# Masks first, small transfers last, turned rows before shifted copies, router steps put off, and weights requested in eight pieces, in a fused attention and expert kernel

## The chip, the cores and the metric

The kernel runs on one core of one Trainium2 chip. The metric is device time in microseconds (us) of one execution. The engines are PE (TensorE matmul; PEld is its weight load), DVE (VectorE), ACT (ScalarE), POOL (GpSimd) and SP (SyncE, which here only issues transfers). L445 is line 445 of the kernel before.

## The reference, cut to what matters

Sliding-window causal attention (8 batches, 8 heads, 576 positions, head width 64, window 64) gives x of 4608 rows by 512. Then each row goes through one of 8 experts.

```
scores = scale * matmul(q, k.T); mask = (rel >= 0) & (rel < 64)
x = softmax(scores masked) @ v            # (8, 576, 512)
logits = x @ w_gate; local = sigmoid(x @ w_local)
for each batch b, in order of s:
    fresh = argmax(logits[b, s])
    e = fresh if s == 0 or local[b, s] < 0.5 else the expert of s - 1
    p = softmax(logits[b, s])
    out[b, s] = p[e] * (relu(x[b, s] @ w1[e]) @ w2[e])
```

The expert of a row depends on the rows before it, so the router scans along the positions, counts the rows of each expert and gives every row a place in a table; the experts then gather their rows by that table.

## The kernel before, in words

**Attention** works through 9 chunks of 512 rows (`sc`), each with 4 units (`hp`, a pair of heads): 36 units, numbered here from 0 to 35. A unit has scores (PE, L389, 36 instructions, into PSUM `sp`), an exponential (ACT, L420), a multiplication by a mask (DVE, L425), values (PE, L435, 32 instructions, into PSUM `xo`), and a normalization on DVE (reciprocal L440, gates L443 in the later chunks, rows `x` L445). Scores run two units ahead of values (`LEAD = 2`). For seven units around chunks 4 to 6 (`BIASED`) a matmul adds the mask to the scores instead, and DVE has no L425. The values need two layouts of v: `va` as loaded and `vb`, shifted by 64 rows, which POOL (L365, L369) and ACT (L364, L367, L371) copy a chunk ahead (`shift`, a generator that gives one piece at a time); for chunk 0 `shift_first` does so in two halves (L379, L380). In chunks 0 to 3 PE turns the finished rows (L306), ACT copies them (L309), and a gate matmul (L319) with L336 and L342 gives the logits `lt`. In chunks 4 to 8 (`GATED`) the gates ride along with the values instead: `gates` and `spread` (L321, L336, L350 to L352) put them beside v. The gates, `spread` and the router share one PSUM bank, `r`.

**Order.** Inside attention the order on PE, ACT and SP is the order written (`manual_schedule`); DVE and POOL are ordered by the framework's scheduler, which may take a later instruction earlier when its data are ready in the scheduler's own model. `issue_after(x)` holds instructions of an engine behind x on that engine.

**Loads.** SP issues all loads. The first chunk's keys, queries and v come first; `until(i, x)` is a tiny transfer that reads x and so holds SP's queue until x is written: the second chunk's loads stand behind `until(0, mask 0)`, the third's behind the first reciprocal. POOL begins with seven small transfers (L117 to L134: gate weights, and zero rows for two DRAM tables), then the iotas for the masks (L260, L267). Mask 0 is built by L279 before the scores of unit 0 are masked, mask 1 behind the masking of unit 1. PE fills its waits at the outset with 12 and then 24 transposes of the identity (L253).

**Router.** `Router.first` handles the first 14 blocks of 128 rows, and runs inside attention from unit 18 on. It is a generator; each `yield w, trip` gives the weight of the step just done and whether the next begins on PE. Every unit has two places for a step (`step()`, ahead of the values and behind them). A place lowers `pause` by 0.8, and when it is at or below zero one step is taken and its weight added. At two places of a unit group (unit 3's first and unit 2's second), where the PSUM bank is in use, a step that begins on PE is not taken. Its steps in order: argmax (L803 to L817), transposes (L823) and a scan along the rows (L828, L829), transposes (L833, L834), carries (L844, L846), experts (L856, L860), counting matmuls (L869, L870) and sums (L872 to L899), the first experts' limits, places (L1040 to L1047 and L928 to L940), and a table: one-hots `rowh` (L968), `one`, `colh`, matmuls (L991), and the row numbers `idx` and `gx` (L993 to L1000). Then POOL gathers the first expert's rows (`ex.rows`, L1176). `Router.second` handles the rest during the first experts; L1126 belongs to it.

**Hand-over.** At the end of unit 27 SP gets the first expert's w1 (four pieces of 512 KB, behind `until(2, ...)`), at the end of unit 29 its w2 (four pieces, behind `until(3, ...)`). After attention PE turns the gathered rows (L1249), ACT copies them (L1250), and the first expert begins (L1473, then L1377). DVE forms sums of w2 (L1290) during its first product.

## Time and profile before

| what | value |
|---|---|
| time, median of 3 runs | 634.47 us (633.39 to 634.62) |
| the profiled execution, its own time | 635.46 us |
| its span, first to last instruction | 633.2 us |
| mean granted TensorE clock | 0.991 |
| PE, PEld, DVE, ACT, POOL busy | 605.1, 532.2, 403.8, 200.8, 271.1 us |
| first expert's first product | 136.43 us |

How to read the lines that follow. A timeline row has: start, duration (us), engine, line, operation, out<-in, shape, xcount, and in brackets the idle time of the engine just before it and what released it. A row that stands for several instructions gives the time from the first to the last. A row of the grouped view has: line, engine, operation, out<-in, xcount | busy us, mean ns | idle us ahead of the group, by releaser. A window row has: from:to, its length, busy us of the engine asked for (xinstructions), granted clock of PE, share of the DMA engines' time, GB/s. "issue" means that nothing the profile shows was waited for.

### The profile page before, as it was taken

How to read it: one execution, taken by the hardware profiler on the slowest of the kernel's cores; microseconds unless marked ns; L12 is line 12 of the kernel's file. 1: busy time of each engine (PE TensorE's matmuls, PEld its weight loads, DVE VectorE, ACT ScalarE, POOL GpSimd, SP SyncE). 2: the span in 40 equal slices, each digit the busy share in tenths (PEclk: the TensorE clock that was granted, in tenths of full speed). 3: DMA queues.
4: the chain of work that ended last, by engine and by line, in shares of the span. 5: the costliest groups of instructions: out<-in, count | busy, mean ns of one | idle time of the engine just before them, and what ended most of it. 6: DMA issues, size and time to landing. Idle time of an engine off the chain costs nothing. (4 is left out here: it accounts for less than half of the span.)

```text
span 633.2 us, 14966 instructions
## 1 busy us (share of the span) xinstructions
PE 605.1 (96%) x6271; PEld 532.2 (84%) x6271; DVE 403.8 (64%) x757; ACT 200.8 (32%) x368; POOL 271.1 (43%) x261
## 2 busy tenths in 40 slices
PE   8889998989999999999999999999999999999994
PEld 7667776878889998979898889888997998989983
DVE  6767579868996767347472785273928752986630
ACT  3756655722382231203130223022211221213120
POOL 5332112525003753446077836182477264574101
PEclk9999989989999999999999999999999999999998
DMA  8999996967945566486967866688689456966401
GB/s 317 412 419 403 382 361 250 322 255 252 376 151 193 194 224 240 168 292 242 384 253 250 293 219 226 212 314 298 275 289 333 182 193 239 370 244 225 166 18 39
DMA packets 31880, 165.79 MB, mean 262 GB/s; under 512 B 10532, under 2 KB 12218, under 8 KB 22587
## 3 DMA queue, kind: packets, MB, share of 16 engines
q1 hardware_dynamic: 20394, 135.54, 57.7%
q0 software_dynamic: 11408, 29.20, 13.1%
q8 instruction: 51, 0.84, 0.5%
q14 instruction: 27, 0.21, 0.1%
HBM read 145.52 MB, written 19.59 MB: 261 GB/s over the span
## 5 line engine op out<-in xcount | busy, mean ns | idle before, releaser
L1176 POOL DMA_INDIRECT xg<-xs,g x118 | 132.9, 1126 | 36.0 <-issue 34.1
L1453 POOL DMA_INDIRECT out_dram<-y,idx x36 | 41.7, 1158 | 179.4 <-DVE y L1386 113.6
L1377 PE MATMUL hp<-ws,hs 128*128 128x256 f32 x384 | 88.9, 380 | 0.0
L1377 PEld LDWEIGHTS hp<-ws,hs 128*128 128x128 f32 x384 | 72.5, 190 | 10.9 <-issue 1.2
L1327 PE MATMUL hp<-xs,ws 128*128 128x128 f32 x672 | 79.7, 275 | 0.0
L1327 PEld LDWEIGHTS hp<-xs,ws 128*128 128x128 f32 x672 | 77.3, 192 | 0.1
L1473 PE MATMUL hp<-xt,w 128*64 128x64 f32 (+2 forms) x640 | 66.2, 276 | 0.0
L1473 PEld LDWEIGHTS hp<-xt,w 128*128 128x128 f32 (+1 forms) x640 | 60.8, 170 | 4.1 <-issue 0.7
L1386 DVE SCALAR_TENSOR_TENSOR y<-hp,pws,kept 128x256 f32<-128x256 f32 x48 | 22.1, 480 | 63.2 <-issue 38.0
L1377 PE MATMUL hp<-w,h 128*128 128x256 f32 x256 | 60.5, 379 | 0.0
L1338 DVE TENSOR_TENSOR h<-hp,keep 128x512 f32<-128x512 f32 x42 | 28.5, 689 | 44.0 <-PE hp L1327 43.9
L1327 PEld LDWEIGHTS hp<-xt,w 128*128 128x128 f32 x448 | 53.2, 192 | 2.7 <-issue 2.3
L1327 PE MATMUL hp<-xt,w 128*128 128x128 f32 x448 | 54.7, 275 | 0.0
L435 PE MATMUL xo<-vb,p 128*64 128x74 f32 (+1 forms) x576 | 46.2, 235 | 8.2 <-DVE x L445 3.5
L1377 PEld LDWEIGHTS hp<-w,h 128*128 128x128 f32 x256 | 47.3, 190 | 5.7
L420 ACT ACTIVATE p<-sp 128x512 f32<-128x512 f32 x72 | 39.2, 595 | 38.5 <-PE sp L389 36.4
L1176 POOL DMA_INDIRECT pws<-xw,gx x40 | 45.4, 1134 | 12.2 <-issue 11.9
L435 PEld LDWEIGHTS xo<-vb,p 128*64 128x64 f32 x576 | 40.6, 143 | 11.0 <-issue 3.8
L389 PEld LDWEIGHTS sp<-w 64*64 64x64 f32 x1296 | 38.6, 137 | 13.3 <-issue 9.8
L425 DVE TENSOR_TENSOR p<-p,mask 128x1024 f32<-128x1024 f32 x29 | 36.4, 1258 | 17.3 <-ACT p L420 17.0
L389 PE MATMUL sp<-w 64*64 64x128 f32 (+1 forms) x1296 | 43.9, 269 | 3.3 <-issue 2.6
L435 PE MATMUL xo<-va,p 128*64 128x74 f32 (+1 forms) x576 | 46.3, 235 | 0.6 <-issue 0.6
(287 smaller groups left out, 966.1 us busy)
## 6 DMA issues: line engine op xcount, KB each, us to landing
w<-in_w_dram SPq DMA_DIRECT2D x22, 2048.0 KB, 9.2
w<-in_w1t_dram SPq DMA_DIRECT2D x20, 2048.0 KB, 8.9
w<-in_kq_dram SPq DMA_DIRECT2D x17, 1024.0 KB, 8.7
w<-in_w_dram SPq DMA_DIRECT2D x24, 512.0 KB, 8.4
xs<-x POOLq DMA_DIRECT2D x9, 1024.0 KB, 7.3
va<-in_v_dram SPq DMA_DIRECT2D x5, 1184.0 KB, 8.0
vtt<-in_vt_dram SPq DMA_DIRECT2D x5, 1024.0 KB, 10.6
va<-in_v_dram SPq DMA_DIRECT2D x3, 1040.0 KB, 13.1
```

The costliest lines, as they stand in the source:

```text
L389: nc.tensor.matmul(sp[j][c * WIN:(c + 1) * WIN, a:b], lhsT=kt[h, hp, block * WIN:(block + 1) * WIN], rhs=qt[h, hp, a:b], start=not biased, ...
L420: nc.scalar.activation(p[:, j], sp[j], Act.Exp, scale=DH ** -0.5)
L425: masked.append(nc.vector.tensor_tensor(p, p, m.to_broadcast([P, 2, SC]), op=Alu.mult))
L435: nc.tensor.matmul(xo[par * WIN:(par + 1) * WIN, j, s * VW:s * VW + n], lhsT=p[:, j, b * WIN:(b + 1) * WIN], rhs=w[:, s, 2 * hp + j, :n], ...
L1176: return self.nc.gpsimd.indirect_dma_start(out=out, out_offset=None, in_=table[:rows, :], in_offset=bass.IndirectOffsetOnAxis(ap=idx, axis=0))
L1327: nc.tensor.matmul(out[:, m, :], lhsT=a[:, kk, m * P:(m + 1) * P], rhs=b[:, kk, :], start=start and m + kk == 0, stop=stop and (m, kk) == ...
L1338: nc.vector.tensor_tensor(o, x, y, op=add)
L1377: nc.tensor.matmul(out, lhsT=a[:, m, :], rhs=b[:, m, :], start=start and m == 0, stop=stop and m == FK // 2 - 1, skip_group_check=True)
L1386: nc.vector.scalar_tensor_tensor(y[i][:, j * w:(j + 1) * w], x, pw[i], y2, Alu.mult, Alu.add)
L1453: self.nc.gpsimd.indirect_dma_start(out=self.out[:, :], out_offset=bass.IndirectOffsetOnAxis(ap=st["idx"][:, s:s + 1], axis=0), in_=y, in_ ...
L1473: nc.tensor.matmul(hp[a, i, :], lhsT=st["w1"][:, kk, m * P:(m + 1) * P][:, a], rhs=st["xt"][:, kk, :n], start=(kk == 0), stop=(kk == DK - 1))
```

## The change: what it does

- **Small transfers.** The seven transfers of POOL go into a function `small()`, called behind unit 2's values and held behind the second half of `shift_first`'s POOL copy.
- **Masks.** Both masks are built at once, ahead of the first scores; `shift_first(0)` stands behind the scores of unit 0 instead of unit 1; the second warm-up has 6 transposes instead of 24.
- **Turned rows.** At unit 0 of chunks 1 to 4 the pieces of `shift` are issued behind the turned rows and their copy, not ahead of them.
- **Router steps.** The scan's step weighs 2.4 instead of 1.5; the second place of unit 3 of a group no longer takes a step that begins on PE; the one-hot `rowh` is made in two halves with a step each; L1126 is held behind attention's last normalization.
- **Weights.** The first expert's w1 goes out in pieces behind units 27, 28, 29 and 30, its w2 behind units 32, 33, 34 and 35, each piece behind that unit's reciprocal.

```diff
@@ kernel
-    nc.gpsimd.dma_start(out=wg2s, in_=wg2)
-    nc.gpsimd.dma_start(out=wgs, in_=wg)
...
-        for i in (ZR, N + 1):
-            nc.gpsimd.dma_start(out=xs[0][i:i + 1, :], in_=zeros[:1])
-            nc.gpsimd.dma_start(out=xw[i:i + 1, :], in_=zeros[:1, :PW])
-        nc.gpsimd.dma_start(out=xw[T1:ZR, :].rearrange("(c p) o -> p c o", p=HF),
-                            in_=zeros[:HF, :n * PW].rearrange("p (c o) -> p c o", c=n))
+        def small():
+            nc.gpsimd.dma_start(out=wgs, in_=wg)
+            nc.gpsimd.dma_start(out=wg2s, in_=wg2)
...
@@ attention
-    build_mask(0)
+    for i in range(2):
+        build_mask(i)
...
     for u in units[:LEAD]:
         ps[u] = scores(*u)
-    shift_first(0)
-    with tc.issue_after(masked[-1].ins):
-        build_mask(1)
-    warm(24)
+        if u == units[0]:
+            shift_first(0)
+    warm(6)
...
-        for _ in range(2 if sc else 4):
-            next(moves, None) if moves else None
+        late_moves = hp == 0 and sc and sc - 1 not in GATED
+
+        def move():
+            for _ in range(2 if sc else 4):
+                next(moves, None) if moves else None
+
+        if not late_moves:
+            move()
...
+        if late_moves:
+            move()
...
-            shift_first(1)
+            second = shift_first(1)
...
+        if i == 2:
+            with tc.issue_after(second.ins):
+                small()
...
-            ex.jobs = [ex.weights({"plain": True}, -1, ("w1",), lambda: until(2, allr[:1, sc, hp, 0, :1]))]
+            ex.jobs = [ex.weights({"plain": True}, -1, (), lambda: until(2, allr[:1, sc, hp, 0, :1]))]
+            ex.piece(ex.jobs[0], "w1", 0)
...
-        step(not (hp == 2 and sc + 1 in GATED))
-        if (sc, hp) == (NSC - 2, 1):
-            ex.weights(ex.jobs[0], -1, ("w2",), lambda: until(3, allr[:1, sc, hp, 0, :1]))
+        step(not (hp >= 2 and sc + 1 in GATED))
+        at = i - (len(units) - 2 * HP)
+        if 0 <= at < 2 * HP and at != HP - 1:
+            until(3 + at, allr[:1, sc, hp, 0, :1])
+            ex.piece(ex.jobs[0], "w1" if at < HP else "w2", at % HP + (at < HP))
@@ Router.gate
-        yield 1.5, True
+        yield 1.5 if part else 2.4, True
@@ Router.table
-                    vec.tensor_tensor(rowh, self.io128.to_broadcast(sh), last(lo[:, b:b + m]).to_broadcast(sh),
-                                      op=Alu.is_equal)
-                    yield 0.15 * m, False
+                    for c in range(0, m, PIECE // 2):
+                        d = min(c + PIECE // 2, m)
+                        sh = [P, d - c, P]
+                        vec.tensor_tensor(rowh[:, c:d], self.io128.to_broadcast(sh),
+                                          last(lo[:, b + c:b + d]).to_broadcast(sh), op=Alu.is_equal)
+                        yield 0.15 * (d - c), False
@@ Router.second
-        vec.tensor_scalar(none, self.rank[:, :C1], 0.0, float(2 * N), Alu.is_lt, Alu.mult)
+        with self.tc.issue_after(self.norm.ins) if self.norm else nullcontext():
+            vec.tensor_scalar(none, self.rank[:, :C1], 0.0, float(2 * N), Alu.is_lt, Alu.mult)
@@ Experts
+    def piece(self, st, name, i):
+        w, a, b = (self.w1[0], DK, F) if name == "w1" else (self.w2, FK, D)
+        if not i:
+            t = self.ring.tile([P, a * b], F32, name="w")
+            st[name] = t.rearrange("p (a b) -> p a b", a=a)
+        m = a // PARTS
+        src = w[bass.ds(st["e"], 1)].rearrange("o p (a b) -> (o p) a b", a=a)
+        self.nc.sync.dma_start(out=st[name][:, i * m:(i + 1) * m], in_=src[:, i * m:(i + 1) * m])
```

## The prediction, made before the changed kernel was run

> **What bounds the kernel now.** I began with the page.

> ```profile
> span 633.2 us, 14966 instructions
> ...
> PE 605.1 (96%) x6271; PEld 532.2 (84%) x6271; DVE 403.8 (64%) x757; ACT 200.8 (32%) x368; POOL 271.1 (43%) x261
> ```

> TensorE (PE) is busy for 96% of the span, so there is little to win in all; a change pays only where PE stands still. The chain of waits, read next, is of no help: it covers only the kernel's tail. The edits lie in the attention stage and its hand-over to the first expert, so I grouped PE's instructions of the first 137 us by line and read what ended their waits.

> ```profile
> L435 PE MATMUL xo<-vb,p 128*64 128x74 f32 (+1 forms) x576 | 46.2, 235 | 8.2 <-DVE x L445 3.5 <-issue 3.0 <-ACT p L309 1.5
> ```

> The last column is the idle time ahead of the group, by releaser. PE does its scores (L389) and values (L435) in one written order, so these waits add up one behind the other. Three names matter: the normalization on DVE (3.5), ACT's copy of turned rows (1.5), and "issue" (3.0), where nothing that the profile shows was waited for. In time order the waits that the edits touch are these:

> ```profile
> 15.09 1.12 PE L389 MATMUL sp<-w 64*64 64x128 f32 x36
> 16.50 1.54 PE L389 MATMUL sp<-w 64*64 64x128 f32 x36 [0.29 <-DMA w<-in_kq_dram]
> ...
> 83.22 0.39 PE L823 MATMUL r<-ident,vk 128*14 128x128 f32 x2 [0.55 <-ACT va L352]
> ...
> 85.59 0.17 PE L833 MATMUL r<-ident,loc 14*1 14x14 f32 x1 [0.94 <-DVE loc L828]
> ...
> 104.96 0.28 PE L435 MATMUL xo<-vb,p 128*64 128x74 f32 x1 [2.53 <-DVE x L445]
> ...
> 130.64 0.28 PE L435 MATMUL xo<-vb,p 128*64 128x74 f32 x1 [2.03 <-issue]
> ...
> 136.43 3.94 PE L1473 MATMUL hp<-xt,w 128*128 128x256 f32 x17
> ```

> The last row is the first expert's first product; where it starts is my yardstick, since from there PE hardly pauses. The windows show a second cost of a pause, the granted clock (PEclk):

> ```profile
> 86.00:90.00 4.00, 4.00 (x75) 0.57 0.98 395
> 130.00:134.00 4.00, 3.36 (x57) 0.57 0.95 382
> ```

> Behind the two pauses at 83 to 86 us, and behind the one that ended at 130.64, the clock was 0.57 over 4 us: 4 x 0.43 = 1.7 us lost each time. Behind the longest pause, which ended at 104.96, it stayed at 1.00 (the row from 101 to 111, below).

> **The outset.** The seven small transfers leave the front of GpSimd's queue, both masks are built before the first scores are masked, and 18 of 36 warm-up transposes go.

> ```profile
> 2.46 0.61 POOL L119 DMA_DIRECT2D wgs<-in_wg_dram  x1
> ...
> 5.73 0.15 POOL L260 IOTA row<- 128x1 int32 x1
> ```

> ```profile
> 7.32 2.57 DVE L279 TENSOR_SCALAR mask<-p,rowf 64x512 f32<-64x512 f32 x4
> ...
> 12.35 2.59 DVE L279 TENSOR_SCALAR mask<-p,rowf 64x512 f32<-64x512 f32 x4
> ```

> Six of the seven run back to back from 2.46 to 5.73, so the iota for the masks comes at least 3.3 us earlier. Mask 0 then starts near 4.0 and both masks, of 2.6 us each, end near 9.2, where mask 0 alone ended at 9.9, and mask 1 no longer sits between the first masking and the first normalization. The first values could start up to 2 us sooner, but the row at 16.50 says what is late next: the scores of unit 4 wait for the second block of keys and queries. Its request is released by the first mask, so it goes out earlier too.

> ```profile
> 10.00:14.00 4.00, 4.00 (x86) 1.00 1.00 340
> 14.00:18.00 4.00, 3.68 (x112) 1.00 1.01 428
> ```

> Were the queue kept as full from 10 to 14 us as behind it (428 GB/s for 340), it would carry 0.35 MB more, worth 0.8 us; and unit 4's 36 matmuls, 1.54 us at 16.50, took 1.12 in the unit before, 0.4 less. Together -1.2 us; the ends are 0 (the queue moves what it moves) and -2.1 (the masks' gain whole). I take the DMA row, since it bounds last. The small transfers now stand behind GpSimd's second copy, ahead of this one:

> ```profile
> 18.99 1.04 POOL L365 COPY vb<-va 64x1040 f32<-64x1040 f32 x1 [4.93 <-DMA va<-in_v_dram]
> ```

> GpSimd idled 4.93 us there and the seven take about 3.9 (3.3 for six, and one more like the first's 0.61): nothing. Their first user, the gates of chunk 0, comes a chunk later. Without that cover this copy would be late, and with it unit 4's values, one for one.

> **Turned rows first.** In chunks 1 to 4 ACT now copies the turned rows (L309) before the shifted values (L364, L367). Example:

> ```profile
> 56.25 0.63 ACT L364 COPY vb<-va 64x520 f32<-64x520 f32 x1
> 56.78 1.17 ACT L367 COPY vb<-va 64x1184 f32<-64x1184 f32 x1
> 57.98 1.01 ACT L309 COPY p<-xo 128x1024 f32<-128x1024 f32 x1
> ```

> L309 moves 1.7 us ahead, more than any of the waits of L435 on it, whose sum is 1.5 us. The exponentials behind the three copies start when they did; the shifted values are needed only a chunk later. -1.5 us (0 to -1.5).

> **Router steps put off.** Each unit of attention has two places where the router may take a step; a step's weight is worked off at 0.8 a place. Weight 2.4 instead of 1.5 for the scan, and no PE step at either place late in a unit group, move the first transposes (L823) from behind chunk 4's last values to the next chunk, and L833 a whole unit behind them. Both PE waits go, and the slow clock behind them: 0.55 + 0.94 + 1.7 = 3.2; I leave 0.5 for a wait on the scan: -2.7 us (-0.5 if the clock falls elsewhere, to -3.2).

> Counting places through to the end, the counting matmuls move from before unit 22's values to behind unit 24's, and the table's matmuls (L991) from before unit 29's values to before unit 32's. Here DVE must be weighed.

> ```profile
> 93.65 0.39 DVE L872 COPY sums<-r 128x224 f32<-128x224 f32 x1
> ...
> 100.22 1.18 DVE L1126 TENSOR_SCALAR none<-rank 128x112 f32<-128x112 f32 x1
> ...
> 118.33 0.17 DVE L1000 TENSOR_SCALAR gx<-at 128x6 uint32<-128x6 f32 x1
> 118.41 1.22 DVE L425 TENSOR_TENSOR p<-p,mask 128x1024 f32<-128x1024 f32 x1
> 119.54 0.20 DVE L440 RECIPROCAL allr<-xo 128x8 f32<-128x8 f32 x1
> ...
> 120.52 1.22 DVE L425 TENSOR_TENSOR p<-p,mask 128x1024 f32<-128x1024 f32 x1
> ```

> From the first to the third of these rows DVE does 48 router instructions; start to next start they sum to 11.0 us. L1126 (1.1) is now kept behind the last normalization, and about 1.0 comes after the table: 8.9 are left to do between unit 24's values and the table. In that stretch DVE also has 7 normalizations of 0.98 (119.54 to 120.52) and 5 maskings of 1.13 (118.41 to 119.54), and two reductions:

> ```profile
> L538 DVE TENSOR_REDUCE lt<-g 128x36 f32<-128x288 f32 x2 | 1.3, 668 | 0.0
> ```

> 8.9 + 6.9 + 5.7 + 1.3 = 22.8 us. PE takes

> ```profile
> 101.08 0.41 PE L404 MATMUL sp<-bias,unit 64*64 64x512 bf16 x4
> ...
> 125.98 0.28 PE L435 MATMUL xo<-va,p 128*64 128x74 f32 x1
> ```

> 24.9 us now from the end of unit 24's values to unit 32's, 22.4 without the wait of 2.53. So DVE becomes the bound of this stretch. When it led before,

> ```profile
> 101.00:111.00 10.00, 9.43 (x30) 1.00 0.57 216
> ```

> it was busy 94%: 22.8 / 0.943 = 24.2, so -0.7 us of the 2.5 (ends -2.5, PE's bound, and +1.5, the same again the other way with DVE idling a tenth). Halving the one-hot (L968) adds one start and lets a normalization in between; that lies inside this bound.

> **The hand-over.** The table gives the first expert's row numbers, which GpSimd gathers.

> ```profile
> 118.79 1.78 POOL L1176 DMA_INDIRECT xg<-xs,gx  x1 [2.61 <-DVE gx L1000]
> 120.88 1.74 POOL L1176 DMA_INDIRECT xg<-xs,gx  x1 [0.30 <-issue]
> ```

> ```profile
> w<-in_w_dram SPq DMA_DIRECT2D x24, 512.0 KB, 8.4
> ...
> xg<-xs,g POOLq DMA_INDIRECT x118, 3.3
> ```

> ```profile
> 115.89 0.51 PE L991 MATMUL r<-colh,rowh 128*128 128x12 bf16 x14
> ```

> ```profile
> 134.96 1.07 ACT L1250 COPY xt<-tp 128x512 f32<-128x512 f32 x2 [5.53 <-issue]
> ```

> Now: table done 116.40, indices 118.50 (2.1 later), second gather issued 120.88 (+2.4), landed 3.3 later as such gathers do, or up to 8.4 as a weight piece does (I take 5.0, nearer the row of the same kind), turned and copied (+1.1). That sums to 10.6 us behind the table, and unit 32's values follow the table at once. Before, this chain ended by 128 and hid under units 29 to 35. PE now takes 136.43 - 125.98 = 10.45 us from unit 32's values to the first expert, of which 10.45 - 2.03 - 1.7 = 6.7 are work, so it will wait 3.9 us at the end: 10.6 instead of 10.45, +0.2 us (-1.6 with a landing of 3.3, +3.6 with 8.4). Spreading the weight requests over eight units may well remove the 2.03 us pause, but that time is given to the gather. The eighth piece goes out some 6 us behind the start of unit 32's values and lands 8.4 later. The first to want it are DVE's sums of the second weights:

> ```profile
> 143.28 1.19 DVE L1290 TENSOR_TENSOR ws<-w 128x1024 f32<-128x1024 f32 x1
> ```

> That is 6.9 us into the first expert, some 17 behind unit 32's values: covered by 3 us, and what exceeds them is paid one for one. Each piece waits on SP's queue for its unit's reciprocal; behind it stand only further pieces and the store of the routing weights, which the first expert needs last.

> A 3.9 us pause may halve the clock: of the three pauses above two did, so 2/3 x 1.7 = +1.1 us (0 to 1.7). [...]

> **Sum.** -1.2 - 1.5 - 2.7 - 0.7 + 0.2 + 1.1 = -4.8 us. The profiled execution took 635.46 us (span 633.2), 1.0 above the median of 634.47; taken off the median: 629.7 us.

> **Rivals.**
> (1) Late indices eat nearly all. If DVE serves normalizations first, the five index instructions come 5 us behind the table instead of 2; the first expert starts 3 us later: 632.7. For it: DVE is the bound just there. Against it: in the trace router work overtakes normalizations (L1126 and the one-hot both ran ahead of the reciprocal that PE waited for).
> (2) Slower: the gather becomes the bound past today's start. The place is the two row gathers; the price is one us for each us that the indices end later than 136.43 - 8.5 = 127.9 on today's clock. They end at 118.50 now, move by 3 units of 22.4 / 8 = 2.8 us (8.4) and gain 6.1 from the terms upstream, so another 7 us of DVE backlog is needed, or upstream gains that fail (4 us) together with a landing of 8.4. Then 637.
> (3) The change does little of what it says: DVE's order is not written out, so router work may overtake normalizations as before (2.53 stays), and the pauses put down to "issue" fall elsewhere; then -1.2 - 1.5 - 2.7 upstream stand against +3.6 of a late landing and +1.1 of clock: 633.8.

> **Chances.** By 0.2%, 1.3 us, a measurement of this kernel can tell a change. Forecast case (623.5 to 632) 0.66, all faster. Rival 1 (632 to 635) 0.17: 0.11 faster, 0.06 same. Rival 2 0.10, slower. Rival 3 0.07: 0.02 faster, 0.04 same, 0.01 slower. Faster 0.79, same 0.10, slower 0.11. The low end takes every favourable bound (-2.1 - 1.5 - 3.2 - 2.5 - 1.6, no clock loss: -10.9): 623.5; the high end takes in rival 1: 634.8.

> **What would show it.** Right: no wait of L435 on L309 in chunks 1 to 4; no slow clock near 86 us; first values before 10.5 us; unit 4's scores near 15.3; L1126 behind the last normalization; table before unit 32's values; a PE wait for the gathered rows ahead of the first expert, which starts between 128 and 134. Wrong: DVE idle between unit 24 and 32 while PE is not waiting for it (the budget is too high), a first expert without a wait for its rows (landing too long), or more than 1 us of change behind the first expert, where I expect none.

## The result, and the profile after

The kernel after takes 643.8 us (median of four executions, 643.26 to 644.39) where the kernel before takes 634.5 in the same measurement: 1.5% slower, ratio 1.015 with a 95% interval of 1.012 to 1.018. The forecast was 629.7, faster.

The page of the kernel after, first its span, then its busy times:

```profile
span 642.1 us, 14941 instructions
...
PE 607.3 (95%) x6253; PEld 532.3 (83%) x6253; DVE 402.4 (63%) x758; ACT 201.0 (31%) x368; POOL 270.0 (42%) x261
```

The work is the same but for the 18 transposes; 8.9 us of span were added. In time order, PE's rows that answer to those of before are these:

```profile
10.49 0.27 PE L440 MATMUL xo<-vb,p 128*64 128x65 f32 x1
...
16.37 0.53 PE L394 MATMUL sp<-w 64*64 64x64 f32 x6 [1.57 <-issue]
17.33 1.11 PE L394 MATMUL sp<-w 64*64 64x128 f32 x34 [0.43 <-ACT p L425]
...
61.70 0.27 PE L440 MATMUL xo<-vb,p 128*64 128x65 f32 x1 [2.71 <-issue]
...
75.28 0.28 PE L440 MATMUL xo<-vb,p 128*64 128x74 f32 x1
...
99.21 0.27 PE L394 MATMUL sp<-w 64*64 64x64 f32 x1 [1.84 <-issue]
...
110.75 0.22 PE L440 MATMUL xo<-vb,p 128*64 128x74 f32 x1 [1.42 <-issue]
...
120.77 0.28 PE L440 MATMUL xo<-vb,p 128*64 128x74 f32 x1 [2.58 <-DVE x L450]
...
124.06 0.28 PE L440 MATMUL xo<-vb,p 128*64 128x74 f32 x1 [0.98 <-DVE x L450]
...
140.28 1.09 PE L1281 MATMUL tp<-ident,xg 128*128 128x128 f32 x4 [4.45 <-DMA xg<-xs,gx]
...
141.64 1.12 PE L1281 MATMUL tp<-ident,xg 128*128 128x128 f32 x4 [0.27 <-DMA xg<-xs,gx]
...
144.86 3.32 PE L1505 MATMUL hp<-xt,w 128*128 128x256 f32 x11
```

(Line numbers of the kernel after: scores L394, values L440, normalization L450, turn of the gathered rows L1281, first expert L1505; 75.28 is the start of unit 16's values.) The first expert starts at 144.86 us instead of 136.43: 8.4 of the 8.9 us are lost ahead of it. The starts of the values of a few units, read from the two timelines, say where (the forecast column sorts the prediction's terms by where in the kernel before the waits and the slow clock lie):

| stretch | before, us | after, us | difference | forecast |
|---|---|---|---|---|
| start to unit 4 | 25.63 | 25.97 | +0.34 | -1.2 |
| unit 4 to 16 | 44.87 | 49.31 | +4.44 | -1.0 (turned copies at 44 and 59 us) |
| unit 16 to 20 | 15.41 | 12.86 | -2.55 | -1.5 (router's waits, the last turned copy) |
| unit 20 to 24 | 13.98 | 14.48 | +0.50 | -1.7 (slow clock behind the router's waits) |
| unit 24 to 32 | 26.09 | 27.93 | +1.84 | -0.7 |
| unit 32 to the first expert | 10.45 | 14.31 | +3.86 | +1.3 (hand-over and clock) |
| behind it, to the end of the span | 496.77 | 497.24 | +0.47 | 0 |

Two stretches make the loss. In each, the first row to look at is a pause of PE.

**The pause ahead of 61.70.** Nothing that the profile shows was waited for ("issue"). Added up by releaser, up to the first expert, these pauses are, before and then after (columns: total us, times, longest):

```profile
PE xo L435 <- issue: 3.6, 4, 2.0
...
PE sp L389 <- issue: 2.6, 3, 1.4
```

```profile
PE sp L394 <- issue: 6.2, 5, 1.8
PE xo L440 <- issue: 5.2, 6, 2.7
PE tp L1281 <- DMA xg<-xs,gx: 4.7, 2, 4.5
PE xo L440 <- DVE x L450: 4.0, 3, 2.6
```

6.2 us became 11.4, and 2.03 of the 6.2 lay behind unit 32: up to there these pauses grew by more than the 4.6 us that were lost. Counted in the trace, the pauses between 28 and 54 us of the kernel before stand 255 to 257 PE instructions apart (a block, in what follows), 126 to 128 matmuls with their weight loads and now and then a wait on a semaphore. In the kernel after, those of 48.11 and 61.70 stand 511 apart, two such blocks. And the list of DMA queues has q8, named `instruction`, with 51 packets of 0.84 MB in all in each of the two traces. Before, a packet of it started between 54.2 and 55.2 us; after, the same one (the eighth from the start) only between 59.2 and 60.2:

```profile
q8 instruction: 1, 0.02, 7.5%
```

```profile
q8 instruction: 1, 0.02, 6.5%
```

What went out just ahead is on SP's queue: a load of 1.18 MB, chunk 5's rows.

```profile
53.74 0.33 SPq L235 DMA_DIRECT2D va<-in_v_dram  x1
```

PE ran on again 2.3 us behind the start of that packet (59.40), and at half clock (columns: from:to, length, PE busy, granted clock, DMA share, GB/s):

```profile
62.00:66.00 4.00, 4.00 (x52) 0.50 1.03 430
66.00:70.00 4.00, 4.00 (x69) 0.78 0.17 68
```

The half clock lasts from 60.94 to 67.77 us, and PE does 6.1 us of work in it, at a loss of 3.0. So the 4.44 us of this stretch are mostly 3.0 of clock and 2.3 more of pauses (5.9 for 3.6), less 1.0 of waits for turned copies.

**The pause ahead of 140.28.** GpSimd asks for the first expert's rows 13.8 us later than before (118.79 then):

```profile
131.05 0.75 POOL L558 DMA_DIRECT2D xs<-x  x1 [9.28 <-DVE x L450]
132.60 1.78 POOL L1198 DMA_INDIRECT xg<-xs,gx  x1 [0.80 <-DVE gx L1021]
134.69 1.74 POOL L1198 DMA_INDIRECT xg<-xs,gx  x1 [0.30 <-issue]
```

The second gather, asked at 134.69, is used at 141.64: 6.95 us. The clock behind it:

```profile
140.00:146.00 6.00, 5.44 (x43) 0.50 0.43 172
```

### The profile page after: what moved, and what is told of

The parts are those of the page before. It is cut to its first block, busy times and chain, and to the rows that moved or that the text cites. A ratio compares the mean times of both kernels' runs of the same rounds, so it can differ in the third digit from the quotient of the medians.

```text
span 642.1 us, 14941 instructions
## 1 busy us (share of the span) xinstructions
PE 607.3 (95%) x6253; PEld 532.3 (83%) x6253; DVE 402.4 (63%) x758; ACT 201.0 (31%) x368; POOL 270.0 (42%) x261
## 5 line engine op out<-in xcount | busy, mean ns | idle before, releaser
L1485 POOL DMA_INDIRECT out_dram<-y,idx x36 | 40.0, 1112 | 183.8 <-DVE y L1418 117.8
L1409 PEld LDWEIGHTS hp<-ws,hs 128*128 128x128 f32 x384 | 72.6, 190 | 10.9 <-issue 1.2
L1505 PE MATMUL hp<-xt,w 128*64 128x64 f32 (+2 forms) x640 | 66.8, 277 | 0.0
L1505 PEld LDWEIGHTS hp<-xt,w 128*128 128x128 f32 (+1 forms) x640 | 61.3, 171 | 4.4 <-issue 0.7
L394 PEld LDWEIGHTS sp<-w 64*64 64x64 f32 x1296 | 40.0, 140 | 18.7 <-issue 14.2
L440 PE MATMUL xo<-vb,p 128*64 128x74 f32 (+1 forms) x576 | 45.8, 232 | 9.0 <-issue 5.0
L394 PE MATMUL sp<-w 64*64 64x128 f32 (+1 forms) x1296 | 45.9, 274 | 7.7 <-issue 6.2
L425 ACT ACTIVATE p<-sp 128x512 f32<-128x512 f32 x72 | 39.2, 595 | 38.2 <-PE sp L394 36.1
L440 PEld LDWEIGHTS xo<-vb,p 128*64 128x64 f32 x576 | 39.8, 140 | 11.7 <-issue 5.7
L1198 POOL DMA_INDIRECT pws<-xw,gx x40 | 44.0, 1101 | 12.2 <-issue 11.6
L430 DVE TENSOR_TENSOR p<-p,mask 128x1024 f32<-128x1024 f32 x29 | 36.1, 1246 | 20.7 <-ACT p L425 20.7
L440 PE MATMUL xo<-va,p 128*64 128x74 f32 (+1 forms) x576 | 46.1, 232 | 0.2 <-issue 0.2
## 6 DMA issues: line engine op xcount, KB each, us to landing
w<-in_w_dram SPq DMA_DIRECT2D x24, 512.0 KB, 5.9
```

The lines of the kernel that those rows point to most:

```text
L394: nc.tensor.matmul(sp[j][c * WIN:(c + 1) * WIN, a:b], lhsT=kt[h, hp, block * WIN:(block + 1) * WIN], rhs=qt[h, hp, a:b], start=not biased, ...
L425: nc.scalar.activation(p[:, j], sp[j], Act.Exp, scale=DH ** -0.5)
L430: masked.append(nc.vector.tensor_tensor(p, p, m.to_broadcast([P, 2, SC]), op=Alu.mult))
L440: nc.tensor.matmul(xo[par * WIN:(par + 1) * WIN, j, s * VW:s * VW + n], lhsT=p[:, j, b * WIN:(b + 1) * WIN], rhs=w[:, s, 2 * hp + j, :n], ...
L1198: return self.nc.gpsimd.indirect_dma_start(out=out, out_offset=None, in_=table[:rows, :], in_offset=bass.IndirectOffsetOnAxis(ap=idx, axis=0))
L1409: nc.tensor.matmul(out, lhsT=a[:, m, :], rhs=b[:, m, :], start=start and m == 0, stop=stop and m == FK // 2 - 1, skip_group_check=True)
```

## The experiments

My theory had two parts. **Fetch:** as I read the pauses 255 to 257 instructions apart and the packets of q8, PE waits there for its next block of instructions; where that block's request falls behind a large load, PE stands still, and what the outset gains is lost. **Gathers:** the put-off router steps bring the first expert's rows too late. The rivals were the outset's new order itself, the eight pieces of weights, and the store in GpSimd's queue.

On the chips of the first three sets and the last one (`best_again` and its neighbours) the time behind the start of the first expert is 44 to 62 us longer, with pauses of its own, and executions of one kernel spread over up to 30 us (one of `after_va_late` took 1246 us); the attention stage runs as on the first chip. The chip of `after_again` and the two runs beside it is as quiet as the first. So I read those runs at the start of the first expert, 136.43 us before and 144.86 after on the first chip, and give ratios beside it. That mark comes from one traced execution of each run, and it has a grain: a stretch of half clock costs about 1.7 us each time (3.41 us at 0.50 in the kernel before), and ahead of the first expert the kernel before has two of them, `outset_alone`, `moves_alone` and `weights_alone` one.

| kernel | unit 16 | unit 32 | first expert | unit 32 to it | ratio to before [95%] |
|---|---|---|---|---|---|
| before (first chip) | 70.50 | 125.98 | 136.43 | 10.45 | 1 |
| after (first chip) | 75.28 | 130.55 | 144.86 | 14.31 | 1.015 [1.012, 1.018] |
| outset_alone | 73.47 | 127.13 | 135.81 | 8.68 | 0.998 [0.993, 1.003] |
| moves_alone | 70.59 | 125.19 | 133.79 | 8.60 | 1.003 [0.998, 1.007] |
| router_alone | 70.34 | 124.93 | 142.06 | 17.13 | 1.007 [1.000, 1.015] |
| weights_alone | 70.40 | 126.38 | 133.41 | 7.03 | 1.000 [0.997, 1.004] |
| after_warm24 | 69.40 | 124.09 | 138.25 | 14.16 | 1.015 [1.012, 1.018] |
| after_old_steps | 69.88 | 124.36 | 131.38 | 7.02 | 0.998 [0.991, 1.005] |
| after_store_late | 73.75 | 129.68 | 143.37 | 13.69 | 1.029 [1.019, 1.038] |
| after_turn_last | 73.62 | 129.36 | 142.40 | 13.04 | 1.019 [1.013, 1.026] |
| before_warm6 | 71.62 | 127.96 | 135.80 | 7.84 | 0.997 [0.992, 1.002] |
| after_va_late | 68.84 | 126.11 | 140.16 | 14.05 | 1.011 [1.005, 1.018] |
| after_again (quiet chip) | 69.86 | 126.56 | 141.30 | 14.74 | 1.014 [1.011, 1.016] |
| after_pieces_held (quiet chip) | 69.41 | 126.55 | 138.87 | 12.32 | 1.008 [1.005, 1.011] |
| after_two_undone (quiet chip) | 68.78 | 126.02 | 133.90 | 7.88 | 0.998 [0.996, 1.000] |
| moves_weights_w18 | 70.31 | 125.24 | 132.27 | 7.03 | 0.990 [0.982, 0.997] |
| best_w18 | 69.55 | 123.30 | 130.33 | 7.03 | 1.001 [0.997, 1.005] |
| best_again | 68.62 | 122.86 | 129.89 | 7.03 | 0.984 [0.975, 0.993] |
| moves_weights_again | 69.75 | 124.98 | 132.01 | 7.03 | 0.988 [0.979, 0.996] |
| best_va_late | 68.33 | 124.26 | 131.65 | 7.39 | 1.002 [0.997, 1.006] |

### Each part alone

The first set makes one part of the change in the kernel before. `outset_alone`:

```diff
-    build_mask(0)
+    for i in range(2):
+        build_mask(i)
...
-    warm(24)
+    warm(6)
...
+        if i == 2:
+            with tc.issue_after(second.ins):
+                small()
```

> The kernel before with the outset's edits alone (masks first, small transfers last, 6 warm-up transposes for 24). Fetch theory: PE reads its instructions in blocks of 256; with the DMA queues full a block comes 2.4 us after its packet starts and PE waits at the block's edge, so a gain at the outset is swallowed by about 25 us, and 36 instructions fewer move each edge, so that the pause of 2.7 us seen near 59 us in the changed kernel comes here too, with 1.7 us of slow clock behind it: 637 to 639 us, unit 16's values 4 us later than in the kernel before. Rival, the waits simply add up (the prediction's own): -1.2 us, 633.3, and no pause near 59 us.

Its first values start at 10.13 us, but it has the pause:

```profile
61.11 0.27 PE L440 MATMUL xo<-vb,p 128*64 128x65 f32 x1 [1.80 <-issue]
```

Unit 16 is 3.0 us late, and the first expert 0.6 early: unit 32 is still 1.2 late, but from there it takes 8.68 us instead of 10.45, though a pause of 1.81 stands there too, because no half clock follows it in this execution. `moves_alone` (turned rows ahead of the shifted copies):

```diff
-        for _ in range(2 if sc else 4):
-            next(moves, None) if moves else None
+        late_moves = hp == 0 and sc and sc - 1 not in GATED
...
+        if late_moves:
+            move()
```

> The kernel before with turned rows copied ahead of the shifted copies, nothing else. Fetch theory: edges stay where they were in the instruction stream; of the 1.5 us of waits for that copy, those at 44 and 59 us lie in the paced stretch and are swallowed, the one at 73 us is kept: -0.5 us, 634.0 (same). Rival, waits add up: -1.5 us, 633.0.

No wait of the values on the turned copy is left at 44, 59 and 73 us, and the first expert is 2.6 us early although this execution began 1.8 us late. These waits are worth 1.5 us; one stretch of half clock less than in the kernel before, 1.7 us, is in the 2.6 too. `router_alone` (scan's step 2.4, slot 3 closed, halved one-hot, L1126 held):

```diff
-        yield 1.5, True
+        yield 1.5 if part else 2.4, True
...
-        step(not (hp == 2 and sc + 1 in GATED))
+        step(not (hp >= 2 and sc + 1 in GATED))
```

> The kernel before with the router's edits alone (scan weight 2.4, second place of unit 3 closed to PE steps, one-hot in halves, L1126 behind the last normalization). Gather theory: the table comes before unit 32's values, the two row gathers land some 7 us after their issue, PE turns the rows ahead of unit 35's values, so the first expert starts 13 to 14 us behind unit 32's values, 3 to 4 us later than in the kernel before, less 2 to 3 us won from the router's own waits near 85 us: 634 to 637. DVE theory: the loss is DVE's backlog at units 29 and 30 (3.6 us), so unit 32 is reached later than at 125.98. The prediction's own: -2.7 - 0.7 + 0.2 + 1.1 = -2.1 us, 632.4.

```profile
138.02 1.94 PE L1252 MATMUL tp<-ident,xg 128*128 128x128 f32 x8 [7.81 <-DMA xg<-xs,gx]
```

It alone brings the late hand-over: unit 32 is 1 us early and the first expert 5.6 late. The second weights still go out in four requests within 3 us here, just ahead of the gathers, and the second gather, issued at 129.08, is used 8.9 us later. `weights_alone` (eight pieces):

```diff
+        at = i - (len(units) - 2 * HP)
+        if 0 <= at < 2 * HP and at != HP - 1:
+            until(3 + at, allr[:1, sc, hp, 0, :1])
+            ex.piece(ex.jobs[0], "w1" if at < HP else "w2", at % HP + (at < HP))
```

> The kernel before with the first expert's weights requested piece by piece behind eight units, nothing else. Fetch theory: the pause of 2.0 us at 128.6 us and the slow clock behind it come from a full DMA queue; with pieces it is mostly empty: -2 to -3.5 us, 631 to 632.5. Rival: the last piece lands too late for DVE's sums of the second weights, or the pause is not the queue's doing: 634 to 636.

The pause of 2.03 us at 130.64 is gone with its half clock, from unit 32 to the first expert it takes 7.03 us, and the first expert is 3.0 us early. So by this mark three parts help or do nothing, and one hurts; none alone has a time that its interval tells from before.

### Fetch: transposes back, the load held

`after_warm24` has the 24 transposes again:

```diff
-    warm(6)
+    warm(24)
```

> The kernel after with 24 warm-up transposes instead of 6, so that TensorE's stream has as many instructions ahead of every unit as the kernel before. Theory F (TensorE's instructions come in blocks of 256 and the block that is due near 54 us is asked for just behind a 1.18 MB load; the 18 transposes taken away shifted the edges): the edges lie where they lay before, the pause of 2.71 us ahead of 61.7 us and the half clock behind it are gone, unit 16's values start near 71 us instead of 75.3 and the kernel is about 4 us below the kernel after, 639 to 640 where before is 634.5. Rival (the pause belongs to the moved transfers and copies and not to where the edges lie): a pause of 2 to 3 us stays near 60 us, unit 16 starts near 75 us, the time is that of the kernel after, 643.8. Second rival (the outset's gain was real and its loss is the price of 18 transposes): 645.

The pause is gone and unit 16 starts at 69.40, 5.9 us earlier than after; what remains late is the hand-over (14.16 us). At the first expert that is 6.6 us better than after; the ratio does not show it. If the count of instructions were all, the kernel before with 6 transposes would get the pause. `before_warm6`:

```diff
-    warm(24)
+    warm(6)
```

> The kernel before with one number changed: 6 warm-up transposes instead of 24 behind the second chunk's mask. Theory F (block edges): 36 instructions fewer ahead of everything put the request for the block that is due near 60 us behind the 1.18 MB load of chunk 5's rows, so the pause of 1.8 to 2.7 us near 61 us that the runs with 6 transposes showed appears here too, unit 16's values start 3 to 4 us later than with 24 (near 74 us instead of 70.5), the first expert near 139 us instead of 136.4. Rival (the pause belongs to the new order of the outset): no pause over 0.9 us near 61 us, unit 16 near 70 us.

It does not: unit 16 starts at 71.62, and near 60 us only the turned copy is waited for (0.82 us). My theory as I had written it fell here: the edge of the block alone is not it. The run is not the count alone either: where transposes stood PE now waits 2.32 us for unit 0's masked scores, the clock is half from 12.27 to 15.68 us, and unit 4 starts 2.1 us late. In this kernel the load went out at 55.30, later than in the kernels with the pause (53.27 to 53.74). What is left is the meeting of the two, and that the next kernel takes away. `after_va_late` keeps everything of the kernel after and holds only that load:

```diff
-        if 0 < sc < NSC - 2 and hp == 0:
+        if 0 < sc < NSC - 2 and hp == (1 if sc == 3 else 0):
+            if sc == 3:
+                until(3 + 2 * HP, allr[:1, sc, 0, 0, :1])
             load(sc + 2, [whole])
```

> The kernel after with one load held: the 1.18 MB of chunk 5's rows, asked at 53.74 us, goes out only when unit 12 is normalized, near 58.7 us. Theory F (the fetch of the next instructions stands behind that load): the pause of 2.71 us ahead of 61.7 us is gone or under 0.7 us, the fetch's packet starts at 55 to 57 us instead of 59.2, unit 16 starts near 70 to 71 us instead of 75.3, the first expert 3 to 5 us earlier than 144.86. Rival (the fetch is late on its own, by its place in the program): the pause stays over 1.8 us and unit 16 at 73.5 to 75.3.

SP's queue shows the load, the DMA queues of 54.2 to 55.2 us the packet, now ahead of it:

```profile
57.41 0.98 SPq L235 DMA_DIRECT2D va<-in_v_dram  x1
```

```profile
q8 instruction: 1, 0.02, 6.7%
```

No pause over 0.2 us is left from 54 to 81 us, and unit 16 starts at 68.84, 6.4 us earlier than after. With the load out of the way the packet comes early, as it would if the fetch had stood behind the load. The yardstick run `after_again`, the kernel after unchanged, shows how fine the meeting is.

> The kernel after, unchanged, as the yardstick of the two kernels that run beside it. Theory (the pause behind the 1.18 MB load and the late gathers belong to the kernel and not to one execution): a pause of 1.8 to 2.8 us near 61 us, unit 16 at 73.5 to 75.5 us, a wait of 4 to 5 us for gathered rows, the first expert at 142.5 to 145 us, 1.2 to 1.8% above before. Rival: the pause comes and goes, unit 16 at 70 us.

```profile
58.61 0.22 PE L440 MATMUL xo<-vb,p 128*64 128x65 f32 x1 [0.33 <-issue]
```

Here the rival was right: this execution has no long pause. Its load went out at 53.18, the packet between 56.2 and 57.2 us. It took 640.27 us; the profiled one with the pause took 643.91. The first experts are 3.56 us apart, the times 3.64. Without the pause the kernel is still 1.0% above before (634.01 on this chip): mostly the gathers' part, since unit 32 comes only 0.6 us late and the hand-over takes 4.3 us longer.

Over all traces with the new outset, the pause near 61 us is in four of the seven executions with 6 transposes and the load not held, in none of the two with 6 transposes and the load held, and in none of the three with 24 transposes and the load not held. So one trace without the pause shows little; the packets' own starts show more. Behind the load the packet came 3.0 and 3.2 us in `after_old_steps` (a pause of 0.36) and here, 1.0 us in `after_pieces_held` (no pause), and 5.3 to 5.7 us in `after`, `outset_alone`, `after_store_late` and `after_turn_last`, with pauses of 1.80 to 2.71. The order goes by how soon the load follows the packet before: where it went out 1.7 to 2.2 us behind that packet, the next packet came 7.0 to 7.7 us behind it (the four with the pause); at 2.2 and 2.3 us, 5.5 and 5.3; at 3.0 us or more, in all other kernels that do not hold the load, 3.7 to 5.5, with no pause of "issue". That a load ahead of the fetch delays it agrees with all of these; why the step near 2.2 us is so sharp stays open.

### Gathers: old steps, store, turn, pieces

`after_old_steps` undoes the router's steps and the halved one-hot in the kernel after; L1126 stays held:

```diff
-        yield 1.5 if part else 2.4, True
+        yield 1.5, True
...
-        step(not (hp >= 2 and sc + 1 in GATED))
+        step(not (hp == 2 and sc + 1 in GATED))
```

> The kernel after with the routing steps as they were: a step of 1.5 behind each scan, steps withheld in slot 2 alone, one-hots built in one piece. Theory G (the put-off steps bring the first expert's indices about 14 us later, and the two gathers that then land late are what PE waits for): the gathers are asked near 119 us, no wait for gathered rows ahead of the last values, the first expert starts 10 to 11 us behind unit 32's values instead of 14.3, and the kernel is 4 to 6 us below the kernel after, 638 to 640. The waits for the router's small transposes near 83 to 86 us come back. Rival (the hand-over is late because the eight pieces of weights fill the DMA engines): the gathers are early but the first expert's weights or rows still come late, 14 us behind unit 32, 643.

```profile
84.37 0.17 PE L851 MATMUL r<-ident,loc 14*1 14x14 f32 x1 [0.92 <-DVE loc L846]
...
131.38 0.92 PE L1502 MATMUL hp<-xt,w 128*128 128x256 f32 x3
```

The router's small waits are back, the gathers are asked at 116.53, nothing waits for them, and the hand-over takes 7.02 us instead of 14.31. More than expected: the put-off steps cost 7.3 us here and save 2.0 between units 16 and 20 (14.81 us, 12.86 in `after`). Unit 16 is 5.4 us earlier than in `after` as well, but that is luck: this execution has no long pause. `after_store_late` asks for the gathers ahead of chunk 7's store:

```diff
+                    with tc.issue_after(ex.jobs[0]["asked"].ins):
+                        while held:
+                            held.pop()()
...
+            if sc == NSC - 2 and side != ():
+                held.append(put)
...
```

> The kernel after with the store of chunk 7's rows (1 MB) placed behind the two gathers of the first expert in GpSimd's queue, instead of ahead of them. If the gathers take 7.5 us to land because they stand behind that store in their own queue: they land 4 to 5 us after their issue, the wait of 4.45 us ahead of the turn goes down to 1 to 2 us, and the kernel is 2.5 to 3.5 us below the kernel after, near 641. If they are slow because the weights' pieces hold the DMA engines: landing stays at 6.5 to 7.5 us, the wait at 3.5 to 4.5, and the time within 1 us of the kernel after.

```profile
136.24 0.63 PE L1290 MATMUL tp<-ident,xg 128*128 128x128 f32 x4 [1.29 <-DMA xg<-xs,gx]
...
140.15 1.12 PE L1290 MATMUL tp<-ident,xg 128*128 128x128 f32 x4 [3.28 <-DMA xg<-xs,gx]
```

The first gather now lands within 4.5 us of its issue (131.73), the second within 6.3 (133.82); the two waits sum to 4.57 us where after has 4.72. The store delays the first gather, but PE needs both. `after_turn_last` puts unit 35's values ahead of the turn on PE:

```diff
+                    rt.fin = nc.tensor.matmul(xo[par * WIN:(par + 1) * WIN, j, s * VW:s * VW + n],
...
-        self.turn(jobs[0], True)
+        with self.tc.issue_after(rt.fin.ins) if rt.fin else nullcontext():
+            self.turn(jobs[0], True)
```

> The kernel after with the turn of the first expert's rows placed behind the last unit's values on TensorE, instead of ahead of them. If PE's order at the hand-over makes the wait dear (the last unit's 32 values stand behind a turn that waits 4.45 us for rows): those values run inside the wait, the first expert starts 1.2 to 2.2 us earlier, near 142.9 us where the kernel after has 144.86, and the kernel is 1 to 2.5 us below the kernel after, 641.5 to 643. Rival (the first expert waits for the turned rows whatever the order): the wait is the same length and starts later by the values' 1.2 us; the first expert starts within 0.5 us of the kernel after, 643.8.

```profile
139.28 0.78 PE L1280 MATMUL tp<-ident,xg 128*128 128x128 f32 x4 [2.52 <-DMA xg<-xs,gx]
...
142.40 2.07 PE L1504 MATMUL hp<-xt,w 128*128 128x256 f32 x4 [0.68 <-ACT xt L1281]
```

The hand-over is 1.27 us shorter, as expected from the order: PE waits 3.06 us for rows instead of 4.72, and unit 35's values run ahead of the half clock. (It varies without any change here, 14.31 us in `after` and 14.74 in `after_again`, so the size is rough.) `after_pieces_held` holds the last three pieces of the second weights until the rows have landed:

```diff
+            rows = ex.jobs[0].get("x") if at >= HP else None
-            until(3 + at, allr[:1, sc, hp, 0, :1])
+            until(3 + at, rows[1][:1, :1] if rows else allr[:1, sc, hp, 0, :1])
```

> The kernel after with the last three pieces of the second weight matrix (1.5 MB, asked at 134.4, 136.5 and 137.7 us) held until the first expert's rows have landed. If the gathers take 7.5 us because these pieces share the DMA engines with them: they land about 5 us after their issue, the wait ahead of the turn is 2 to 3 us in all instead of 4.7, the first expert starts 2 us nearer to unit 32's values (12.3 us behind them instead of 14.3). If the gathers' own length or what was asked before them (the 1 MB store, the piece of 129.2 us) sets it: the wait stays at 4 us or more and the first expert 14 us behind unit 32's values.

```profile
134.12 0.85 PE L1281 MATMUL tp<-ident,xg 128*128 128x128 f32 x4 [2.29 <-DMA xg<-xs,gx]
...
135.65 0.69 PE L1281 MATMUL tp<-ident,xg 128*128 128x128 f32 x2 [0.68 <-DMA xg<-xs,gx]
```

The second gather, issued at 130.68, is used at 135.65: 4.97 us, the forecast's 5.0. In `after_again`, on the same chip, it is issued at 130.71 and used at 138.08: 7.37 us. The hand-over is 12.32 us for 14.74, the waits 2.97 in all for 5.08, and the profiled execution took 638.28 us for 640.27, both without the long pause. So the pieces, asked while the gathers run, make them land late.

### Both undone, and better versions

`after_two_undone` is the kernel after with the load held and the old steps, 6 transposes kept (both diffs above).

> The kernel after with its two collisions taken away and its 6 warm-up transposes kept: the 1.18 MB load held until unit 12 is normalized, and the routing steps as they were. Theory (those two are the whole loss): no pause over 0.7 us near 61 us, unit 16 at 69 to 70.5 us, gathers asked near 116 to 119 us and no wait for them, the first expert at 129.5 to 131.5 us, 5 to 7 us ahead of where the kernel before has it (136.43) and 13 to 15 us ahead of the kernel after; the time 0.6 to 1% below before, unless the experts' stage swallows it. Rival (a third loss is hidden in the sum): the first expert at 134 us or later.

The time is 632.74 us, 10.2 below the kernel after on the same chip (`after_again`, 642.92) and 0.2% below before (ratio 0.9977, interval 0.9958 to 0.9995). Unit 16 is early (68.78) and the gathers wait for nobody, but another pause has come:

```profile
90.82 0.28 PE L440 MATMUL xo<-va,p 128*64 128x74 f32 x1 [2.75 <-issue]
```

With it the first expert starts at 133.90, 2.4 us behind the range that I expected. Fetch pauses of 1.3 to 2.2 us near 88 to 92 us are also in `after_va_late`, `after_store_late`, `after_turn_last`, `after_pieces_held` and `after_again`: so the rival's third loss looks like the first one at another place. In `after_two_undone` the block's packet starts at 88.06, 6.7 us behind another load of 1.18 MB (81.35); no run holds that load, so this is not shown.

`moves_weights_w18` and `best_w18` give the scan 1.8 instead of 2.4: the small transposes come one unit later, the table stays ahead of unit 29.

```diff
-        yield 1.5, True
+        yield 1.5 if part else 1.8, True
```

The first has the moves and the weights beside it, the second the outset (with 24 transposes) and the held L1126 too.

> The kernel before with the turned rows ahead of the shifted copies, the weights in eight pieces, and a scan's step of 1.8 instead of 1.5 (2.4 in the kernel after): the router's small transposes come one unit later, but the table stays ahead of unit 29 where the kernel before has it. Outset, slots and one-hots as before. Theory: no waits for the turned copies at 44, 59 and 73 us, none for the router's transposes near 83 to 86 us, gathers early; first expert at 130 to 132 us where before has 136.43, so 4 to 6 us below before. Rival (gains in the attention are swallowed elsewhere, as in the four parts alone): the first expert is earlier and the time within 1.5 us of before.

> The same with the new order of the outset and its 24 warm-up transposes kept, and the one-off flag behind the last normalization. Theory: as the kernel just named, and the first values start near 10.5 us, but PE is paced by instruction fetch from 16 to 62 us so that little of that is left: first expert at 129.5 to 131.5 us, 5 to 7 us below before. Rival (the outset's gain of 1.2 us carries through): 1 us or more below the kernel just named.

Their first experts start at 132.27 and 130.33 us, 4.2 and 6.1 ahead of before, the second as expected and the first 0.3 us outside its range; a wait of 1.0 us for the scan's carry has come in place of that of 0.94 for its first results. Neither has half clock ahead of the first expert, where the kernel before lost 3.3 us by it. The ratios do not agree with the marks, so I ran both again, and the second with the load held.

> The kernel best_w18, unchanged (new outset with 24 warm-up transposes, turned rows ahead of the shifted copies, weights in eight pieces, flag behind the last normalization, a scan's step of 1.8), for a time where the experts' stage has no pauses of its own. Theory (what the first expert's start gains reaches the end): first expert near 130.3 us, 6 us ahead of the kernel before, and a time 5 to 7 us below before, ratio 0.989 to 0.993. Rival (the gain is given back later): ratio 0.996 or more with the first expert as early. Second rival (it was luck with the fetch): first expert at 133 us or later.

> The kernel moves_weights_w18, unchanged (outset of the kernel before). Theory: first expert near 132 us and a time 3.5 to 5 us below before, ratio 0.992 to 0.9945; so 1 to 2 us above the kernel best_w18, which is what the outset is worth with its transposes kept. Rival (the outset is swallowed by the fetch): within 0.7 us of it.

> The kernel best_w18 with the 1.18 MB load held until unit 12 is normalized. Theory (that load only matters where a fetch falls behind it, and with 24 transposes it does not): unit 16 at 69 to 70 us as without the hold, the time within 1 us of best_w18. Rival (the hold helps every kernel): unit 16 before 68.5 us and 1 to 2 us below best_w18. Second rival (the hold makes the loads behind it late): 1 us or more above it.

The marks repeat: 129.89, 132.01 and, with the hold, 131.65 us. The ratios were 0.984 [0.975, 0.993], 0.988 [0.979, 0.996] and 1.002 [0.997, 1.006], on a noisy chip again. So the second kernel is 1.9 and 2.1 us ahead of the first at the first expert. By unit 16, where the outset has to show, it is 0.8 and 1.1; the rest comes later, where the pauses of "issue" lie otherwise (and L1126 differs too), so it is not shown to be the outset's. The hold is of no use here: unit 16 comes 0.3 to 1.2 us earlier, but a pause of 1.73 follows at 75.91, and the first expert is 1.3 to 1.8 us later. How much of the 6 us reaches the end was not settled: `best_w18` never ran on the quiet chip.

## Why the prediction was wrong, step by step

**What bounds the kernel.** I named "issue" as one of three waits and did not ask what it was. I now read it as the fetch of instructions, by the 255 to 257 instructions between the pauses and a packet 2.3 to 2.6 us ahead of the end of each, and between 16 and 62 us, with the DMA engines full (1.01 of their time in both kernels), PE stopped at nearly every block (from 28 to 54 us for 0.24 to 1.36 us each before, for 0.41 to 1.13 after). Terms that I summed there came only in part: in `after_warm24` unit 16 starts 1.1 us earlier than before, where the terms ahead of it sum to 2.2.

**The outset, -1.2: failed.** The first values came at 10.49 as forecast, but unit 4's scores at 16.50 (the last two of the row at 16.37), behind 1.57 us of "issue", not at 15.3. The step that failed is the one with no price on it: "18 of 36 warm-up transposes go". Together with the earlier outset they brought a late fetch, behind a load as far as the runs show: +4.4 us from unit 4 to 16 in the measured execution. With the transposes kept, the outset gave 0.8 and 1.1 us by unit 16, the size that I had forecast.

**Turned rows, -1.5: right.** The waits on the copy, 1.5 us, are gone from the kernel after and with the edit alone.

**Router steps, -2.7: right where I put it, wrong in what it moved.** Unit 16 to 20 gained 2.55 us where the waits of this step and the last turned copy were to bring 1.5, and no slow clock followed. Its 1.7 us lie between units 20 and 24, and a fetch pause of 1.84 at 99.21 ate them: together these stretches gained 2.05 of 3.2. The table moved behind unit 31 as I had counted.

**DVE's stretch, -0.7: wrong sign, +1.84.** Of the 1.84 us, 0.7 are waits for DVE (3.56 us, 2.88 before) and 0.8 are pauses of "issue" (1.42, at 110.75, for 0.64). I let DVE interleave evenly. Its rows in the kernel after:

```profile
113.69 0.68 DVE L450 TENSOR_TENSOR x<-xo,allr 128x512 f32<-128x512 f32 x1
...
114.36 1.55 DVE L989 TENSOR_TENSOR rowh<-io,lo 128x640 bf16<-128x640 f32 x2
115.83 1.18 DVE L994 TENSOR_TENSOR one<-ios,hi 128x60 bf16<-128x60 f32 x1
116.94 1.66 DVE L989 TENSOR_TENSOR rowh<-io,lo 128x512 bf16<-128x512 f32 x1
118.53 1.21 DVE L430 TENSOR_TENSOR p<-p,mask 128x1024 f32<-128x1024 f32 x1
```

From a normalization at 113.69 to the next masking at 118.53 stand 4.2 us of one-hots in one block, and PE waits 2.58 us at 120.77. Halving the one-hot let nothing in between. This is what my third rival had said of DVE's order.

**The hand-over, +0.2 and +1.1 of clock: mis-sized, 3.86.** The chain was right up to the second gather's issue: from the end of the table (130.62) to 134.69 are 4.1 us, forecast 4.5. The landing took 6.95 instead of 5.0, because pieces that I had spread "over eight units" went out while the gathers ran (`after_pieces_held`). And from the second turn to the first expert are 3.22 us, not 1.1: I left out unit 35's values, which stand behind the turn on PE (2.17 us at half clock; `after_turn_last`). Taken as work, waits and clock, the forecast was 6.7, 3.9 and 1.1; the kernel after has about 7.1, 5.0 and 2.2. The work was nearly right, since kernels without late gathers and pauses take 7.0; the wait and the clock were too small.

**The rivals.** The second named the mechanism: gathers that bound, by upstream gains that fail together with a long landing. I held both failing at once for unlikely (0.10) and priced it at 637. What cost most upstream, a late fetch ahead of unit 16, is in none of the three. Upstream did not only fail to gain, it lost 4.6 us by unit 32.

## What to carry to other kernels

Pauses of "issue" that stand an equal count of instructions apart (255 to 257) were here, as I read them, the engine waiting for its own code; while the DMA queues are full, look for what is asked just ahead of the next block before counting any gain in that stretch. A step that is put off pays with its whole chain down to the last consumer, here a gather that must land before the next stage, while transfers spread over the same units made that gather land 2.4 us later (7.37 us for 4.97). An edit that changed the number of instructions on an engine moved the pauses against the work (those that end at 28.33 us before and at 29.23 after each stand behind 476 matmuls, and 18 of those before are transposes that the kernel after lacks), and such an edit should not be priced at nothing.

## What the runs showed of the hardware

Waiting for instructions cost PE time, if I read the pauses of "issue" right: from 28 to 54 us of the kernel before they stand 255 to 257 PE instructions apart, and a packet of q8 starts 2.4 to 2.6 us ahead of the end of each. They are 0.2 to 2.75 us each up to the first expert, 11.4 us in sum in the kernel after.

```profile
57.53:60.94 3.41, 1.46 (x49) 1.00 1.00 364
60.94:64.35 3.41, 2.65 (x19) 0.50 1.03 433
64.35:67.77 3.42, 3.42 (x52) 0.50 0.66 272
...
115.55:118.97 3.42, 2.64 (x86) 1.00 0.24 96
118.97:122.38 3.41, 1.61 (x50) 1.00 0.19 24
122.38:125.79 3.41, 2.43 (x70) 1.00 0.96 366
```

Of the pause of 2.71 us, 1.95 fall into one such stretch and half clock follows; the 2.58 us fall into two, 0.78 and 1.80. But the idling in one stretch does not settle it either. In the kernel before, counted in the same steps, half clock follows 1.54 us of it (82.63 to 86.04) and 1.80 (127.00 to 130.41), and full clock follows 1.85 (103.11 to 106.52). What decides no run here shows. Pauses of 1.8 to 2.7 us thus cost 1.7 us, 3.0 or nothing behind them here, and their length did not tell which.
